# Dividing the second layer at column 256 instead of 384 in a softcap attention and soft-MoE kernel

## The chip, the cores and the metric

The kernel runs on one core of one Trainium2 chip. The metric is the device time of one execution in microseconds; several runs are taken and their median counts. Beside the runs there is one execution under the hardware profiler, whose span reaches from the first to the last instruction of the program.

## The reference

Eight batches of twelve heads run an attention with capped scores; its output, 3584 tokens of 768 columns, goes through a soft mixture of eight experts with four slots each.

```python
scores = scale * np.matmul(q, k.transpose(0, 1, 3, 2))   # 8 x 12 heads, 448 x 448, head_dim 64
scores = cap * np.tanh(scores / cap)
attn = softmax(scores)
x = (attn @ v) as [3584, 768]

logits = x @ phi                                  # 32 slots
slot_input = softmax(logits over tokens).T @ x    # 32 x 768
for e in range(8):
    h = np.maximum(slot_input[e] @ w1[e], 0.0)    # 4 x 1024
    slot_out[e] = h @ w2[e]                       # 4 x 768
out = softmax(logits over slots) @ slot_out       # 3584 x 768, float32
```

## The kernel before

The kernel writes the order of every engine out by hand. Its first part, some 236 us, is the attention in 56 chunks: scores on PE, tanh and exp on ACT (some of the exps as a polynomial on DVE), the products with v on PE, and the slot logits and slot sums batch by batch. Beside it POOL issues the loads of the weights, 64 jobs (`wjobs`, L123 to L131), one or two in a chunk at slot "b" (L849). The first 32 are w1, which stays on chip. The other 32 are w2, cut by columns into two halves of 384 (`HD`) and by rows into 16 pieces of four blocks: 11 pieces of the first half (`KEPT`) go to the on-chip tile `w2b`, and the other 21 are converted to bf16 in HBM (`w2d`), since there is no room for them until the attention's buffers are free. In `wjobs` all of `w2d` stands before `w2b`. From the end of the attention on, SP loads the 21 pieces from `w2d` into tiles `w2t` (L1047 to L1050), each as soon as the attention buffers under it are free.

The part behind the attention goes by these steps:

- `layer1` and `relu` (L1064 to L1079): the hidden layer of experts 0 to 3 and of 4 to 7, into `hb`. Four matmuls with 32 columns of weights each run side by side on PE.
- `h_transp` (L1081): eight small matmuls turn `hb` into a PSUM tile, and DVE copies it into `hpad` (L1091). Its first call serves the first 32 of the 64 blocks of layer 2, its second the last 32. The second call is made behind 16 blocks of layer 2; `widen` (L1110), which spreads the slot weights `E` of a batch for a later transpose, and `e_recips` (L745), which makes the reciprocals `winv` of two batches, stand behind it in DVE's order.
- `layer2` (L1095): 64 matmuls for the first half of the columns into the PSUM tile `so_ps0`, copied to `so[0]` by ACT (L1158), then 64 for the second half into `so_ps1`, copied to `so[1]` by DVE (L1167).
- `half_tile` (L1132): for one tile of 128 tokens the product of its transposed slot weights with one half of `so` (L1138), scaled by `winv` into a buffer `obh` by ACT or DVE in turn, and stored by SP. `NH = 10` tiles leave in two halves: the first half of eight of them is made between the matmuls of the second half of layer 2, a pair behind every second group of four blocks, so that their stores run while PE works.
- The other 18 tiles are made whole (L1185 to L1199): two matmuls of 384 columns, one scaling of 768 by ACT or DVE, and stores of two to four tiles, whose rows are contiguous in HBM over the tiles.

`bank` (L943) gives PSUM banks by the list `turns`; the buffers `hb`, `so`, `obh` and `ob` take turns in the eight 12 KB slots of w1. All stores and the loads of `w2t` go through SP's one queue.

Of the kernel before, what the change touches and what calls it, by code (L numbers as in the profile page):

```python
# [9 lines left out]
F32 = mybir.dt.float32  # L10
BF16 = mybir.dt.bfloat16
# [7 lines left out]
P = 128  # L19
HP = 64  # L20
NT = 7
DH = 64
S = 448
CH = 6
CS = 3
NG = 4
# [11 lines left out]
def kernel(  # L38
# [12 lines left out]
    B, H, _, _ = q.shape  # L51
    D = H * DH
    E = moe_w1.shape[0]
    F = moe_w1.shape[2]
    NS = moe_phi.shape[1]
    NJ = D // P
    HD = D // 2
    NFT = F // P
    cap = float(cap)
    qk_scale = 1.0 / (DH ** 0.5)  # L60
# [27 lines left out]
    winv = consts.tile([P, B // 2, NT], F32, name="winv")  # L88
# [28 lines left out]

    def load_half(dst, n0, half):
        src = w2_src(n0, 4)
        pool.dma_start(out=dst, in_=bass.AP(tensor=src.tensor, offset=src.offset + half * HD,  # L120
                                            ap=[[D, P], [F * D, 4], [1, HD]]))

    wjobs = [(load_w1, e, jh, fh) for e in range(E) for jh in range(2) for fh in range(2)]  # L123
    w2_parts = [(n0, half) for half in range(2) for n0 in range(0, len(blocks), 4)]
    w2_kept, w2_spilled = w2_parts[:KEPT], w2_parts[KEPT:]

    dram = ctx.enter_context(tc.tile_pool(name="dram", bufs=1, space=bass.MemoryType.DRAM))
    w2d = {part: dram.tile([P, 4, HD], BF16, name=f"w2d{part[0]}_{part[1]}")
           for part in w2_spilled}
# [464 lines left out]
    c0, c1, c3 = POW2  # L594
# [115 lines left out]
    es, wides = {}, {}  # L710
# [25 lines left out]
    def et_tile(bb, c):  # L736
        return (ETl if bb == B // 2 - 1 else ET4[:, bb])[:, c, :, :].rearrange("p a q -> p (a q)")
# [7 lines left out]
    def e_recips(b):  # L745

        sums = zdiag[:, b % 2, 0:NG]
        dve.tensor_reduce(sums, es[b], axis=mybir.AxisListType.X, op=ALU.add)
        to = slice(b % 2 * HP, b % 2 * HP + HP)
        for odd in range(2):  # L750
            dve.reciprocal(winv[to, b // 2, odd:NT:2],
                           sums[odd * HP:odd * HP + HP, 0:(NT + 1 - odd) // 2])
# [63 lines left out]
    for b in range(B):  # L816
        j, p = b * PER, 6 * b
# [226 lines left out]
    tl = ctx.enter_context(tc.tile_pool(name="tl", bufs=1, reuse_waits="tile"))  # L1044

    w2t = {}
    for n0, half in sorted(w2_spilled, key=lambda x: (x[1], x[0])):  # L1047
        t = tl.tile([P, 4, HD], BF16, name=f"w2t{n0}_{half}")
        sp.dma_start(out=t, in_=w2d[n0, half])
        w2t[n0, half] = t  # L1050

    hpad = tl.tile([P, E, NFT, NS], BF16, name="hpad")
    pool.memset(hpad, 0.0)
# [21 lines left out]
    def relu(eng, dst, hp):  # L1075
        if eng is act:
            act.activation(dst, hp, ACT.Relu, scale=rz)
        else:
            dve.tensor_scalar(dst, hp, rz, 0.0, ALU.mult, ALU.max)  # L1079

    def h_transp(i):  # L1081

        own = bass.AP(tensor=ident.tensor, offset=ident.offset + 16 * i,
                      ap=[ident.ap[0], [36, 4], [1, 4]])
        src = psT.tile([P, NFT, 4, 4], F32, name="hps", tag="T")
        for ft in range(NFT):
            pe.matmul(src[:, ft, :, :], hbs[i][:, ft * P:(ft + 1) * P], own,
                      start=(ft == 0), stop=(ft == NFT - 1), skip_group_check=True)
        dst = bass.AP(tensor=hpad.tensor, offset=hpad.offset + i * (4 * NFT * NS + 16),
                      ap=[hpad.ap[0], [NS, NFT], [NFT * NS + 4, 4], [1, 4]])  # L1090
        dve.tensor_copy(dst, src)  # L1091

    so_ps = []
# [10 lines left out]
    for eng, hp in zip((act, dve), first):  # L1104
        relu(eng, *hp)
    relu(act, *layer1(1, 0, 512))
    room = [wts.tile([P, HD + NG * P], BF16, name=f"so{half}", tag="w1", bufs=E) for half in range(2)]
    so = [t[:, 0:HD] for t in room]

    def widen(b):  # L1110

        wides[b] = room[b % 2][:, HD:]
        dve.tensor_copy(wides[b].rearrange("p (g a s) -> p g a s", g=NG, s=NS),
                        es[b].unsqueeze(2).to_broadcast([P, NG, P // NS, NS]))

    widen(B - 1)
    h_transp(0)
    relu(dve, *layer1(1, 512, 768))
    relu(act, *layer1(1, 768, F))
    so_ps += [bank([P, HD], name=f"so_ps{half}") for half in range(2)]  # L1120
    obs, waiting = {}, {}

    def store(n, h0, h1, src, tokens=1):
        bb, c = divmod(n, NT)
        width = (h1 - h0) * HD
        sp.dma_start(out=bass.AP(tensor=out.tensor,
                                 offset=(2 * bb * S + c) * D + h0 * HD,
                                 ap=[[NT * D, P], [1, tokens * D]] if width == D else
                                 [[NT * D, P], [D, tokens], [1, width]]),
                     in_=src)  # L1130

    def half_tile(n, half, home, eng):  # L1132

        bb, c = divmod(n, NT)
        if c == 0:
            obs[bb, half] = wts.tile([P, NT, HD], F32, name="obh", tag="w1", bufs=E)
        ob = obs[bb, half][:, c, :]
        pe.matmul(home, et_tile(bb, c), so[half], start=True, stop=True)  # L1138
        if eng == "dve":
            dve.tensor_scalar_mul(ob, home, winv[:, bb, c:c + 1])  # L1140
        else:
            act.mul(ob, home, winv[:, bb, c:c + 1])
# [4 lines left out]
        store(k, half, half + 1, obs[bb, half][:, c - (n - k):c + 1, :], n - k + 1)  # L1147
# [10 lines left out]
    act.copy(so[0], so_ps[0])  # L1158
# [8 lines left out]
    dve.tensor_copy(so[1], so_ps[1])  # L1167
    for n, eng in ((NH - 2, "act"), (NH - 1, "dve")):
        half_tile(n, 0, bank([P, HD], name="op0"), eng)
    mid.close()  # L1170


    fin = ctx.enter_context(tc.tile_pool(name="fin", bufs=3, space=PSUM, reuse_waits="tile"))
    for n in range(B // 2 * NT):
        bb, c = divmod(n, NT)
        if n == NH + 3:
            e_transp(B - 1)
        if n == NH + 5:
            e_transp(B - 2)
# [12 lines left out]
        if n % 2:  # L1192
            dve.tensor_scalar_mul(dst, op[:, :, 0:HD], winv[:, bb, c:c + 1])
        else:
            act.mul(dst, op[:, :, 0:HD], winv[:, bb, c:c + 1])
        full = n + 1 == n1 + size
        if full:
            store(n1, 0, 2, ob[:, 0:n - n1 + 1, :, :].rearrange("p t a d -> p (t a d)"),
                  n - n1 + 1)  # L1199


# [33 lines left out]
```

## Time and profile before

| | |
|---|---|
| median of 3 runs (lowest to highest) | 281.91 us (281.11 to 282.01) |
| span of the profiled execution | 279.2 us |
| busy in the span: ACT, PE, DVE, POOL | 89%, 88%, 86%, 51% |
| granted PE clock, mean | 0.985 |
| SP's queue (loads of v and w2t, all stores) | 32.02 MB, 32.6% of 16 DMA engines' span |
| POOL's queue (q, k, weights) | 35.31 MB, 80.0% |

The page gives no other time of the profiled execution than its span. Engine rows say where an engine is busy; the windows view cuts the span into stretches and gives each engine's busy time, the number of its instructions, and in the last two columns the busy share of the 16 DMA engines and their rate. Since a DMA's time is counted where its packet starts, a share can pass 1. A timeline row is a run of like instructions on one engine: start, length from the first start to the last end, line, operation, tiles with shapes, count, and in brackets the idle time ahead of it.

### The profile page before, as it was taken

What the parts mean: (1) busy time and instruction counts of PE and PEld (TensorE: products, weight loads), DVE (VectorE), ACT (ScalarE), POOL (GpSimd) and SP (SyncE); (2) the same over time, 40 slices, a digit from 0 to 9 for tenths busy, and PEclk for the clock granted to TensorE, in tenths of its full rate; (3) what the DMA queues carried; (4) which work ended last, traced back from release to release, by engine and by line L of the source; (5) the groups of instructions that cost most, each with busy time, mean ns of one, the idle gap of its engine ahead of it and who ended that gap; (6) DMA issues with size and microseconds to landing.
All of it is one profiled execution on the core that took longest, in us unless ns stands there. A gap on an engine that the chain in (4) does not pass through costs nothing.

```text
span 279.2 us, 10421 instructions
## 1 busy us (share of the span) xinstructions
PE 247.0 (88%) x4560; PEld 166.6 (60%) x4560; DVE 239.1 (86%) x473; ACT 248.6 (89%) x195; POOL 142.0 (51%) x198
## 2 busy tenths in 40 slices
PE   8898989998999999989999999899999999998720
PEld 7555556756675766566756675657566678553300
DVE  3479999999999999999999999999999997347940
ACT  4999999999999999999999999999999998237720
POOL 8796548662957296728673758375743230200000
PEclk9999999999999999999999999999999999999995
DMA  6999999999999999999999999999999588979997
GB/s 197 277 193 202 219 219 234 229 221 219 224 225 220 219 229 226 225 217 229 223 226 212 213 219 231 218 210 215 231 217 215 117 279 293 367 290 383 434 424 312
DMA packets 57340, 68.08 MB, mean 244 GB/s; under 512 B 4048, under 2 KB 53840, under 8 KB 56784
## 3 DMA queue, kind: packets, MB, share of 16 engines
q0 software_dynamic: 42448, 35.31, 80.0%
q1 hardware_dynamic: 14704, 32.02, 32.6%
q8 instruction: 35, 0.57, 0.7%
q10 hardware_dynamic: 144, 0.10, 0.1%
q14 instruction: 9, 0.07, 0.1%
HBM read 91.72 MB, written 19.27 MB: 398 GB/s over the span
## 4 chain that ended last, share of the span: by engine, by line
ACT 38%; DVE 27%; PE 27%; issue 3%; POOL 1%; ACTq 0%; DVEq 0%
ACT ex L366 15%; ACT ex L374 15%; PE pv L627 8%; ACT ex L362 6%; DVE xq L637 4%; PE sc L349 3%; DVE xp L605 3%; DVE xp L607 3%; DVE ex L608 2%; DVE ex L602 2%; PE so_ps L1098 2%; PE hp L1070 2%; DVE xf L604 2%; DVE ex L609 2%; DVE xp L606 2%
## 5 line engine op out<-in xcount | busy, mean ns | idle before, releaser
L366 ACT ACTIVATE ex<-sc 128x1344 f16<-128x1344 f32 (+1 forms) x87 | 112.9, 1402 | 0.9 <-PE sc L349 0.9
L374 ACT ACTIVATE ex<-ex 128x1344 bf16<-128x1344 f16 (+5 forms) x58 | 110.7, 1916 | 0.1
L627 PE MATMUL pv<-vbd,ex 128*128 128x130 bf16 (+1 forms) x1610 | 94.0, 212 | 7.6 <-POOL vbd L289 3.4
L627 PEld LDWEIGHTS <-ex 128*128 128x128 bf16 (+1 forms) x1680 | 75.6, 101 | 34.9 <-issue 6.2
L289 POOL CAST vbd<-vraw 64x896 bf16<-64x896 f32 x46 | 47.3, 1028 | 57.3 <-PE pv L627 35.7
L349 PE MATMUL sc<-qT,kT 64*64 64x448 bf16 x672 | 66.0, 359 | 6.7 <-ACT ex L366 4.8
L362 ACT ACTIVATE ex<-sc 128x2688 f16<-128x2688 f32 x13 | 33.6, 2586 | 0.0
L349 PEld LDWEIGHTS <-kT 64*64 64x64 bf16 x672 | 22.1, 105 | 16.3 <-ACT ex L366 6.9
L637 DVE TENSOR_TENSOR xq<-pv,rec 128x448 bf16<-128x448 f32 x46 | 28.7, 625 | 1.6
L607 DVE TENSOR_TENSOR xp<-xp,xf 128x1344 f16<-128x1344 f16 (+2 forms) x34 | 27.1, 798 | 0.6
L608 DVE TENSOR_TENSOR ex<-ex,xp 128x1344 uint16<-128x1344 uint16 (+2 forms) x34 | 26.9, 791 | 0.2
L605 DVE TENSOR_TENSOR xp<-xf 128x1344 f16<-128x1344 uint16 (+2 forms) x34 | 26.8, 789 | 0.2
L116 POOL DMA_DIRECT2D w1b<-in_moe_w_dram x32 | 26.3, 825 | 0.0
L602 DVE TENSOR_SCALAR ex<-ex 128x1344 uint16<-128x1344 f16 (+2 forms) x34 | 17.0, 500 | 1.4 <-ACT ex L366 0.8
L606 DVE TENSOR_SCALAR xp<-xp 128x1344 f16<-128x1344 f16 (+2 forms) x34 | 17.2, 505 | 0.6
L281 DVE COPY kT<-kps 128x896 bf16<-128x896 bf16 x23 | 14.2, 617 | 4.0 <-PE kps L276 2.8
L297 POOL MEMSET vbd<- 64x1 bf16 x22 | 2.8, 129 | 28.6 <-PE pv L627 28.3
L604 DVE TENSOR_SCALAR xf<-ex 128x1344 uint16<-128x1344 uint16 (+2 forms) x34 | 16.7, 491 | 0.4
L185 POOL DMA_DIRECT2D qb<-in_q_dram x22 | 16.3, 740 | 1.2 <-PE qps L279 0.5
L609 DVE TENSOR_SCALAR ex<-ex 128x1344 uint16<-128x1344 uint16 (+2 forms) x34 | 16.4, 483 | 0.4
L120 POOL DMA_DIRECT2D w2d<-in_moe_w_dram x21 | 16.4, 816 | 0.0
L185 POOL DMA_DIRECT2D kb<-in_k_dram x22 | 16.3, 739 | 0.0
(124 smaller groups left out, 320.2 us busy)
## 6 DMA issues: line engine op xcount, KB each, us to landing
w1b<-in_moe_w_dram POOLq DMA_DIRECT2D x32, 384.0 KB, 10.2
vraw<-in_v_dram SPq DMA_DIRECT2D x44, 224.0 KB, 6.2
w2d<-in_moe_w_dram POOLq DMA_DIRECT2D x21, 384.0 KB, 9.9
w2t<-w2d SPq DMA_DIRECT2D x21, 384.0 KB, 6.2
qb<-in_q_dram POOLq DMA_DIRECT2D x22, 224.0 KB, 8.2
kb<-in_k_dram POOLq DMA_DIRECT2D x22, 224.0 KB, 8.1
w2b<-in_moe_w_dram POOLq DMA_DIRECT2D x11, 384.0 KB, 9.5
out_dram<-ob SPq DMA_DIRECT2D x2, 1536.0 KB, 7.7
```

The source lines that it names most:

```text
L116: pool.dma_start(out=w1b[e][:, js, fs], in_=w1r[:, e, js, fs])
L185: pool.dma_start(out=t, in_=quad_ap(nm, Q))
L289: pool.tensor_copy(vbds[Q % 2][r, :, :, c0:c0 + DH], raw[r])
L349: ins = pe.matmul(sc[cs, u, 0:S], qkT["k", Q][r, c, cs], qkT["q", Q][r, :, cs], start=True, stop=True).ins
L362: apart["t", i - 1] = apart["t", i] = act.activation(exs[j].bitcast(F16), own["board"][:, :, 0:S], ACT.Tanh, scale=qk_scale / cap).ins
L366: ins = act.activation(exs[j][:, half * CS + u0:half * CS + u1, :].bitcast(F16), (own[0] if i == u0 == 0 else sc)[:, u0:u1, 0:S], ACT.Tanh ...
L374: act.activation(exs[j][:, u0:u1, :], exs[j][:, u0:u1, :].bitcast(F16), ACT.Exp, scale=cap)
L605: lambda: dve.tensor_tensor(p, s, s.bitcast(F16), op=ALU.mult),
L607: lambda: dve.tensor_tensor(p, p, s, op=ALU.mult),
L608: lambda: dve.tensor_tensor(y, y, p, op=ALU.add),
L627: pe.matmul(out_, exs[j][r, u, q0:q0 + (HP if tail else P)], v_, start=(c == 0 and g == gs[0] < NF), stop=(c == NT - 1), skip_group_check= ...
L637: dve.tensor_tensor(xq[Q][:, h, s0:s1, :], pv[:, 0:s1 - s0, 0:DH], rec.to_broadcast([P, s1 - s0, DH]), op=ALU.mult)
```

## The change

Layer 2 is divided at column 256: `WD` is (256, 512). The first part's 16 weight pieces all stay on chip in `w2b` (16 x 256 columns instead of 11 x 384), the second part's 16 all go through HBM (16 x 512 instead of 21 x 384), and in `wjobs` the two kinds alternate. Both parts of `so` lie side by side in one buffer, so that the whole tiles still take two matmuls of 384. Sixteen tiles (`NH`) instead of ten leave in two parts; the first parts of all sixteen are made inside layer 2's second part, a pair behind each of the groups 2 to 9; stores of both parts are made for pairs of tiles, with a buffer of seven tiles for the first part and of four for the second. The second `widen` and the two `e_recips` move ahead of layer 2, and the copy of `so_ps1` is cut between DVE and ACT.

```diff
+    CUTS = (0, D // 3, D)
+    WD = tuple(CUTS[n + 1] - CUTS[n] for n in range(2))
-    KEPT = 11
-    w2b = wts.tile([P, KEPT, 4, HD], BF16, name="w2b")
+    w2b = wts.tile([P, E * NFT // 4, 4, WD[0]], BF16, name="w2b")
...
-    wjobs += [(load_half, w2d[part], *part) for part in w2_spilled]
-    wjobs += [(load_half, w2b[:, n, :, :], *part) for n, part in enumerate(w2_kept)]
+    for n in range(len(w2_kept)):
+        wjobs.append((load_half, w2d[w2_spilled[n]], *w2_spilled[n]))
+        wjobs.append((load_half, w2b[:, n, :, :], *w2_kept[n]))
...
-    turns = [0, 1, 2, 6, 3, 4, 5, 0, 6, 0, 1, 2, 3, 6, 5, 4, 0, 1, 2, 6, 3, 0, 1, 2, 6, 5]
+    turns = [0, 1, 2, 6, 3, 4, 5, 0, 6, 0, 1, 2, 3, 6, 5, 4] + [0, 1, 2, 6, 3, 5] * 4
...
-        t = tl.tile([P, 4, HD], BF16, name=f"w2t{n0}_{half}")
+        t = tl.tile([P, 4, WD[1]], BF16, name=f"w2t{n0}_{half}")
...
-    room = [wts.tile([P, HD + NG * P], BF16, name=f"so{half}", tag="w1", bufs=E) for half in range(2)]
-    so = [t[:, 0:HD] for t in room]
+    room = [wts.tile([P, D + NG * P], BF16, name=f"so{half}", tag="w1", bufs=E) for half in range(2)]
+    so = [room[0][:, CUTS[n]:CUTS[n + 1]] for n in range(2)]
...
+    GR = (NT, 4)
-    def half_tile(n, half, home, eng):
+    def part_tile(n, half, home, eng):
...
-        if c == 0:
-            obs[bb, half] = wts.tile([P, NT, HD], F32, name="obh", tag="w1", bufs=E)
-        ob = obs[bb, half][:, c, :]
+        g, u = divmod(c, GR[half])
+        if u == 0:
+            obs[bb, half, g] = wts.tile([P, GR[half], WD[half]], F32, name="obh", tag="w1", bufs=E)
+        ob = obs[bb, half, g]
...
-        if half and 0 < n < NH - 1 and c < NT - 1 and k == n:
+        if 0 < n < NH - 1 and u < GR[half] - 1 and c < NT - 1 and k == n:
...
-    NH = 10
+    NH = 16
+    widen(B - 2)
+    for b in (B - 2, B - 1):
+        e_recips(b)
     for n0 in range(0, n2, 4):
         if n0 == n2 // 2 - 16:
             h_transp(1)
-            widen(B - 2)
-            for b in (B - 2, B - 1):
-                e_recips(b)
         layer2(n0, 0)
     act.copy(so[0], so_ps[0])
     done = 0
     for n0 in range(0, n2, 4):
         layer2(n0, 1)
-        if n0 % 8 == 4 and n0 > 4 and done < NH - 2:
+        if n0 and done < NH:
             for eng in ("act", "dve"):
-                half_tile(done, 0, bank([P, HD], name="op0"), eng)
+                part_tile(done, 0, bank([P, WD[0]], name="op0"), eng)
                 done += 1
-    dve.tensor_copy(so[1], so_ps[1])
-    for n, eng in ((NH - 2, "act"), (NH - 1, "dve")):
-        half_tile(n, 0, bank([P, HD], name="op0"), eng)
+    dve.tensor_copy(so[1][:, 0:WD[1] // 2], so_ps[1][:, 0:WD[1] // 2])
+    act.copy(so[1][:, WD[1] // 2:], so_ps[1][:, WD[1] // 2:])
...
-        if n == NH + 3:
+        if n == 13:
-        if n == NH + 5:
+        if n == 15:
...
-            half_tile(n, 1, op[:, 0, 0:HD], "dve" if n % 2 else "act")
+            part_tile(n, 1, op[:, 0, 0:WD[1]], "dve" if n % 2 else "act")
...
-            pe.matmul(op[:, half, 0:HD], et_tile(bb, c), so[half],
+            pe.matmul(op[:, half, 0:HD], et_tile(bb, c), room[0][:, half * HD:half * HD + HD],
```

The change moves instructions at three places that matter below. The first is DVE's order around the second copy into `hpad`; `hps` is the turned hidden layer, `E` the slot weights of a batch, and the COPY into a tile `so` is `widen`. Before:

```order
L1091 CAST hpad<-hps 128x8x4x4
L1079 TENSOR_SCALAR hb<-hp,rz 128x256
L1091 CAST hpad<-hps 128x8x4x4
L1113 COPY so_5878<-E 128x512
L748 TENSOR_REDUCE zdiag<-E 128x4
L751 RECIPROCAL winv<-zdiag 64x4
L751 RECIPROCAL winv<-zdiag 64x3
```

and with the change:

```order
L1092 CAST hpad<-hps 128x8x4x4
L1080 TENSOR_SCALAR hb<-hp,rz 128x256
L1114 COPY so_5863<-E 128x512
L749 TENSOR_REDUCE zdiag<-E 128x4
L752 RECIPROCAL winv<-zdiag 64x4
L752 RECIPROCAL winv<-zdiag 64x3
L749 TENSOR_REDUCE zdiag<-E 128x4
L752 RECIPROCAL winv<-zdiag 64x4
L752 RECIPROCAL winv<-zdiag 64x3
L1092 CAST hpad<-hps 128x8x4x4
```

Seven instructions that stood behind the second CAST into `hpad` now stand ahead of it; PE's matmuls of blocks 32 to 63 read what that CAST writes.

The second place is DVE's order between the two copies of layer 2's results, where `op` is the PSUM tile of a tile's product and the CAST is the copy of `so_ps1`. Before:

```order
L1140 TENSOR_SCALAR obh<-op_6048,winv 128x384
L1140 TENSOR_SCALAR obh<-op_6064,winv 128x384
L1140 TENSOR_SCALAR obh<-op_6080,winv 128x384
L1140 TENSOR_SCALAR obh<-op_6096,winv 128x384
L1167 CAST so_5879<-so_ps_5944 128x384
L1140 TENSOR_SCALAR obh<-op_6130,winv 128x384
```

and with the change:

```order
L1144 TENSOR_SCALAR obh<-op_6025,winv 128x256
L1144 TENSOR_SCALAR obh<-op_6036,winv 128x256
L1144 TENSOR_SCALAR obh<-op_6047,winv 128x256
L1144 TENSOR_SCALAR obh<-op_6058,winv 128x256
L1144 TENSOR_SCALAR obh<-op_6070,winv 128x256
L1144 TENSOR_SCALAR obh<-op_6081,winv 128x256
L1144 TENSOR_SCALAR obh<-op_6092,winv 128x256
L1144 TENSOR_SCALAR obh<-op_6104,winv 128x256
L1171 CAST so_5863<-so_ps_5929 128x256
```

Eight pairs of tiles (DVE has one of each pair, ACT the other) instead of four now stand ahead of the copy; the fifth pair before stood behind it. The third place is ACT's order around its new half of that copy, with the semaphores that each instruction waits for:

```order
L1146 ACTIVATE obh<-op_6077,winv 128x256 [waits PE_49]
L1146 ACTIVATE obh<-op_6088,winv 128x256 [waits PE_49]
L1146 ACTIVATE obh<-op_6100,winv 128x256 [waits DMASW3_49,DMASW1_49,DMASW5_49,DMASW0_49,PE_49]
L1172 CAST so_5863<-so_ps_5929 128x256 [waits DVE_49]
L1146 ACTIVATE obh<-op,winv 128x512 [waits DMASW5_49,DMASW6_49,DMASW0_49,DMASW7_49,PE_49,Pool_49]
```

ACT had no instruction here before; its half of the copy waits for DVE, whose last instruction ahead of it is the other half of the same copy.

More of the change, by code (lines that the diff above doesn't have):

```diff
@@ L119, in load_half @@
         src = w2_src(n0, 4)
-        pool.dma_start(out=dst, in_=bass.AP(tensor=src.tensor, offset=src.offset + half * HD,
-                                            ap=[[D, P], [F * D, 4], [1, HD]]))
+        pool.dma_start(out=dst, in_=bass.AP(tensor=src.tensor, offset=src.offset + CUTS[half],
+                                            ap=[[D, P], [F * D, 4], [1, WD[half]]]))
     wjobs = [(load_w1, e, jh, fh) for e in range(E) for jh in range(2) for fh in range(2)]
-    w2_parts = [(n0, half) for half in range(2) for n0 in range(0, len(blocks), 4)]
-    w2_kept, w2_spilled = w2_parts[:KEPT], w2_parts[KEPT:]
+    w2_kept, w2_spilled = ([(n0, half) for n0 in range(0, len(blocks), 4)] for half in range(2))
     dram = ctx.enter_context(tc.tile_pool(name="dram", bufs=1, space=bass.MemoryType.DRAM))
-    w2d = {part: dram.tile([P, 4, HD], BF16, name=f"w2d{part[0]}_{part[1]}")
+    w2d = {part: dram.tile([P, 4, WD[1]], BF16, name=f"w2d{part[0]}_{part[1]}")
            for part in w2_spilled}
-    wjobs += [(load_half, w2d[part], *part) for part in w2_spilled]
-    wjobs += [(load_half, w2b[:, n, :, :], *part) for n, part in enumerate(w2_kept)]
+    for n in range(len(w2_kept)):
+        wjobs.append((load_half, w2d[w2_spilled[n]], *w2_spilled[n]))
+        wjobs.append((load_half, w2b[:, n, :, :], *w2_kept[n]))
     att = ExitStack()
@@ L1106 @@
     relu(act, *layer1(1, 0, 512))
-    room = [wts.tile([P, HD + NG * P], BF16, name=f"so{half}", tag="w1", bufs=E) for half in range(2)]
-    so = [t[:, 0:HD] for t in room]
+    room = [wts.tile([P, D + NG * P], BF16, name=f"so{half}", tag="w1", bufs=E) for half in range(2)]
+    so = [room[0][:, CUTS[n]:CUTS[n + 1]] for n in range(2)]
     def widen(b):
-        wides[b] = room[b % 2][:, HD:]
+        wides[b] = room[b % 2][:, D:]
         dve.tensor_copy(wides[b].rearrange("p (g a s) -> p g a s", g=NG, s=NS),
@@ L1119, with store @@
     relu(act, *layer1(1, 768, F))
-    so_ps += [bank([P, HD], name=f"so_ps{half}") for half in range(2)]
+    so_ps += [bank([P, WD[half]], name=f"so_ps{half}") for half in range(2)]
     obs, waiting = {}, {}
-    def store(n, h0, h1, src, tokens=1):
+    def store(n, c0, c1, src, tokens=1):
         bb, c = divmod(n, NT)
-        width = (h1 - h0) * HD
+        width = c1 - c0
         sp.dma_start(out=bass.AP(tensor=out.tensor,
-                                 offset=(2 * bb * S + c) * D + h0 * HD,
+                                 offset=(2 * bb * S + c) * D + c0,
                                  ap=[[NT * D, P], [1, tokens * D]] if width == D else
@@ L1130, in store @@
                      in_=src)
-    def half_tile(n, half, home, eng):
+    GR = (NT, 4)
+    def part_tile(n, half, home, eng):
         bb, c = divmod(n, NT)
-        if c == 0:
-            obs[bb, half] = wts.tile([P, NT, HD], F32, name="obh", tag="w1", bufs=E)
-        ob = obs[bb, half][:, c, :]
+        g, u = divmod(c, GR[half])
+        if u == 0:
+            obs[bb, half, g] = wts.tile([P, GR[half], WD[half]], F32, name="obh", tag="w1", bufs=E)
+        ob = obs[bb, half, g]
         pe.matmul(home, et_tile(bb, c), so[half], start=True, stop=True)
         if eng == "dve":
-            dve.tensor_scalar_mul(ob, home, winv[:, bb, c:c + 1])
+            dve.tensor_scalar_mul(ob[:, u, :], home, winv[:, bb, c:c + 1])
         else:
-            act.mul(ob, home, winv[:, bb, c:c + 1])
+            act.mul(ob[:, u, :], home, winv[:, bb, c:c + 1])
         k = waiting.pop(half, n)
-        if half and 0 < n < NH - 1 and c < NT - 1 and k == n:
+        if 0 < n < NH - 1 and u < GR[half] - 1 and c < NT - 1 and k == n:
             waiting[half] = n
             return
-        store(k, half, half + 1, obs[bb, half][:, c - (n - k):c + 1, :], n - k + 1)
-    NH = 10
+        store(k, CUTS[half], CUTS[half + 1], ob[:, u - (n - k):u + 1, :], n - k + 1)
+    NH = 16
     n2 = len(blocks)
+    widen(B - 2)
+    for b in (B - 2, B - 1):
+        e_recips(b)
     for n0 in range(0, n2, 4):
@@ L1197 @@
         if full:
-            store(n1, 0, 2, ob[:, 0:n - n1 + 1, :, :].rearrange("p t a d -> p (t a d)"),
+            store(n1, 0, D, ob[:, 0:n - n1 + 1, :, :].rearrange("p t a d -> p (t a d)"),
                   n - n1 + 1)
```

## The prediction

> **What bounds the kernel now.** I read the engine rows first (ACT and PE are both near nine tenths until 236 us), then the chain of waits, then stretches of the tail one by one, because everything that the change rewrites on the engines lies behind 245 us. The stretches show that the tail has another limit than the attention:
>
> ```profile
> core 0: us, PE busy (x) PEld busy (x) DVE busy (x) ACT busy (x) POOL busy (x), PEclk, DMA share, GB/s
> 248.50:249.90 1.40, 1.40 (x27) 0.39 (x20) 0.29 (x1) 0.98 (x2) 0.00 (x0) 1.00 0.36 137
> 249.90:250.80 0.90, 0.90 (x15) 0.26 (x12) 0.72 (x2) 0.61 (x2) 0.00 (x0) 1.00 0.01 3
> 250.80:254.50 3.70, 3.46 (x44) 1.26 (x42) 2.64 (x6) 2.03 (x5) 0.00 (x0) 1.00 1.04 387
> 254.50:255.00 0.50, 0.16 (x2) 0.10 (x1) 0.50 (x1) 0.50 (x2) 0.00 (x0) 1.00 0.83 307
> 255.00:260.50 5.50, 4.86 (x27) 2.25 (x26) 4.90 (x10) 4.62 (x7) 0.00 (x0) 1.00 1.05 392
> 261.00:264.50 3.50, 2.45 (x14) 1.17 (x13) 2.81 (x4) 2.59 (x3) 0.00 (x0) 1.00 1.03 429
> 261.00:277.80 16.80, 4.59 (x23) 1.93 (x21) 6.45 (x7) 5.30 (x6) 0.00 (x0) 0.80 0.99 419
> 277.80:279.20 1.40, 0.00 (x0) 0.00 (x0) 0.00 (x0) 0.00 (x0) 0.00 (x0) 0.50 0.00 0
> ...
> 249.98 8.86 SPq L1126 DMA_DIRECT2D out_dram<-obh  x16
> 259.08 9.57 SPq L1126 DMA_DIRECT2D out_dram<-ob  x6
> ```
>
> The last two columns are the 16 DMA engines' busy share and rate; the last two rows are SP's store issues. The first store is issued at 249.98 and its data moves from 250.8, 0.82 us later. From there the DMA engines are full until 277.8, with one small dip at 254.5, and the span ends 1.4 us behind. Issuing ends at 268.65, so DVE, ACT and PE have some 9 us of slack at the end. The tail is therefore a stream of 11.0 MB (3584 x 768 x 4 bytes), and its end is: when it starts, plus its bytes at the rate of their pieces, plus every hole in it. That is the account in which I put the change. The page's span is 279.2 us, the runs' median 281.91; I add the difference of the spans to the median.
>
> **Rate by piece.** A stored row of a 384-column half is 1536 bytes: 392 GB/s at share 1.05, so 16 x 1536 / (392/1.05) = 65.8 ns on one DMA engine. The two-token stores of 261.0 to 264.5 have rows of 6144 bytes: 16 x 6144 / (429/1.03) = 236 ns. Two points give 9.1 ns per piece plus 0.0369 ns per byte. Estimates from that at share 1.05 and 1.04: pieces of 1024 bytes (256 columns) 46.9 ns, 367 GB/s; of 2048 bytes (512 columns) 84.7 ns, 402 GB/s. [...]
>
> **Part by part.** Weights through HBM: 21 loads of 384 KB become 16 of 512 KB, 1.6% more bytes; the buffers on chip come free at the same events.
>
> ```profile
> L1049 SPq DMA_DIRECT2D w2t<-w2d x21: 319/371/1539, 222.2 to 242.5; - x21
> DMA to landing us min/median/max: 3.0/6.2/8.5
> ...
> L120 POOL DMA_DIRECT2D w2d<-in_moe_w_dram x21: 696/774/992, 112.1 to 174.3; - x21
> L120 POOL DMA_DIRECT2D w2b<-in_moe_w_dram x11: 740/760/834, 180.5 to 212.8; - x11
> ...
> PE sc L349 <- ACT ex L366: 4.6, 9, 0.7
> PE pv L627 <- POOL vbd L289: 3.2, 7, 0.7
> ...
> PE sc L349 <- DVE qT L281: 0.4, 2, 0.3
> ```
>
> The last is issued at 242.5 and lands by 251 at the latest; its last reader now runs at about 255 (below), so PE's second part hides the loads and I cost them at nothing; without that cover each late microsecond would be one of the end. On POOL the 32 jobs stay 32 at the same places; 774 and 760 ns an issue are one price, and a job of 512 KB instead of 384 is followed by one of 256. In the attention PE's wait list (8 rows, first and last shown) names no DMA, so I cost the mixed order at nothing too, bounds -0.3 and +0.5 us, nearest to nothing.
>
> First part of layer 2, 256 columns instead of 384:
>
> ```profile
> 239.63 4.07 PE L1070 MATMUL hp<-w1b,slT 128*32 128x512 bf16 x72
> 243.92 1.49 PE L1070 MATMUL hp<-w1b,slT 128*32 128x256 bf16 x48
> ...
> 246.00 0.36 PE L1087 MATMUL hps<-ident,hb 128*128 128x16 bf16 x8
> 246.28 1.32 PE L1098 MATMUL so_ps<-w2b,hpad 128*32 128x384 bf16 x28
> 247.43 1.64 PE L1098 MATMUL so_ps<-w2t,hpad 128*32 128x384 bf16 x36
> 249.00 0.50 PE L1138 MATMUL op<-so,ET 128*128 128x384 bf16 x2
> 249.43 0.51 PE L1098 MATMUL so_ps<-w2t,hpad 128*32 128x384 bf16 x8
> 249.87 0.50 PE L1138 MATMUL op<-so,ET 128*128 128x384 bf16 x2
> 250.30 0.51 PE L1098 MATMUL so_ps<-w2t,hpad 128*32 128x384 bf16 x8
> ...
> 244.81 0.48 DVE L1079 TENSOR_SCALAR hb<-hp,rz 128x256 bf16<-128x256 f32 x1 [0.43 <-PE hp L1070]
> 246.39 0.29 DVE L1091 CAST hpad<-hps 128x128 bf16<-128x128 f32 x1 [1.10 <-PE hps L1087]
> 246.60 0.28 DVE L1113 COPY so<-E 128x512 bf16<-128x512 bf16 x1
> ...
> 247.80 0.36 DVE L751 RECIPROCAL winv<-zdiag 64x4 f32<-64x4 f32 x2
> 253.25 0.56 DVE L1167 CAST so<-so_ps 128x384 bf16<-128x384 f32 x1 [0.48 <-PE so_ps L1098]
> ...
> 248.47 0.48 ACT L1158 CAST so<-so_ps 128x384 bf16<-128x384 f32 x1 [2.53 <-PE so_ps L1098]
> 249.38 0.58 ACT L1142 ACTIVATE obh<-op,winv 128x384 f32<-128x384 f32 x1 [0.42 <-PE op L1138]
> ...
> L1077 ACT ACTIVATE hb<-hp,rz 128x512 bf16<-128x512 f32 x2 | 1.4, 688 | 4.3 <-PE hp L1070 4.3
> L1077 ACT ACTIVATE hb<-hp,rz 128x256 bf16<-128x256 f32 x1 | 0.5, 475 | 1.0 <-PE hp L1070 1.0
> ```
>
> Four matmuls run side by side as a group. With one drain of 0.16 us at the end of each run, the rows of 72, 48 and 36 matmuls give 0.217 us a group at 512 columns (18 groups), 0.111 at 256 (12) and 0.164 at 384 (9), in proportion to the columns. The second transpose at 246.00 hangs on ACT's relu and stays; behind it 12 groups are left, 12 x 0.053 = 0.64 us less. But the moved widen and reciprocals now stand ahead of DVE's CAST into hpad, which the last eight groups read. They take 246.60 to 248.16, 1.56 us, and can start when the relu ends at 245.29 (DVE is idle 1.10 us there now): to 246.85, CAST to 247.14, PE on at 247.19 instead of 246.28 + 4 x 0.111 = 246.72, a new stall of 0.47 us (bounds 0.2, if they start earlier, and 0.6). Eight groups and the drain end at 248.24; ACT's copy loses 0.11 (a third of 384 columns at the slope of ACT's two relu rows, 0.213 us per 256): 248.29 to 248.66; tile 0 starts at 248.71 instead of 249.00, its matmul ends at 248.98, ACT (475 ns) at 249.50, the store goes out at 249.52 and moves data at 250.34: **0.46 us earlier**.
>
> Second part. Before, a pair of 384-column tiles stands behind every second group, four pairs in all, and a cycle is 0.87 us (249.43 to 250.30): 2 x 0.164 for the groups, 2 x 0.17 for the tiles, 0.2 for the two changes between them. Now eight pairs stand behind single groups of 512 columns: 0.217 + 2 x 0.12 + 0.2 = 0.65 us. The eighth pair starts at 248.71 + 7 x 0.65 = 253.26, takes 0.33 (0.43 less two thirds of 0.16), seven groups follow (1.52), and the drain: so_ps is whole at **255.3 instead of 253.25**. Bounds for the changes: nothing (0.45 a cycle, 1.6 us less) and what an old cycle costs (0.87, 1.5 more); the price of the old changes is nearest, as the same two matmul shapes meet.
>
> The copy in two. DVE's 256 columns take 0.56 less 0.11, by ACT's slope, ACT's 0.48 less 0.11; as the order shows, ACT's half waits for DVE's, so with two hops the pair is 0.9 us, not 0.45 (the two bounds). [...] Then: tile 0 of the second part at 256.2, matmul 0.38, ACT 0.69 (688 ns), issued 257.3, **data at 258.15**.
>
> The hole. The first part is 16 x 128 KB = 2.10 MB: 5.7 us at 367 GB/s, and 0.25 lost behind the lone first store (the next needs another cycle). From 250.34 it runs dry at **256.3**. Before, ten larger pieces (1.97 MB) reached to 255.8 and the next came in time. So the engines idle 1.85 us. Behind it lie 16 x 256 KB at 402 GB/s, 10.4 us, and 12 whole tiles, 4.72 MB at 419 GB/s, 11.3 us: 279.85, and 1.4 to the span's end: 281.25. ACT writes a tile of 512 columns in 0.69 us beside DVE, while a pair's stores last 1.3 us, so nothing starves again; the slack of 9 us shrinks by two. SP's 23 stores instead of 22 cost nothing: 16 of them took 8.86 us, 0.55 each, under the 0.7 us or more of data in a pair. Buffers that are written again wait for stores issued at least six before them, which the hole lets land.
>
> **Sum against 279.2:** start -0.46, hole +1.85 instead of about 0.1, lone-store gap +0.25, pieces (5.7 + 10.4 + 11.3 = 27.4 against 26.9) +0.5: **+2.0 us**. The hops between engines are rounded up, so I take +1.9: 281.91 + 1.9 = **283.8 us**.
>
> **Rivals.** (1) The stream stays whole: PE changes between shapes for nothing and the weights of so come 1.85 us earlier. Then 250.34 + 0.25 + 27.4 + 1.4 = 279.4, **282.1 us**: no change. For it: the old dip was only 0.5 us long. Against it: the 0.87 us cycles. (2) Faster: the stream is whole and small pieces cost no more, so 27.0 us count from 250.34: 278.7, **281.4 us**; this mechanism needs the second part's first data by 256.3 and is decided there. [...] (3) The larger HBM loads come late, or the mixed order delays k and q: the last load must come over 4 us after 251 to matter, and the end moves by as much as it passes 255; with the +0.5 of the mixed order and 1.2 of lateness **285.5 us**. (4) The cycle stays at 0.87: so_ps at 256.8, **285.3 us**.
>
> **Chances.** Forecast 0.70, rival (1) 0.12, (2) 0.08, (3) 0.05, (4) 0.05. What a measurement here can tell from no change is about 0.3%, 0.85 us. Faster 0.09, same 0.15 (rival 1 and the forecast's lower edge), slower 0.76. Own range of the forecast 282.9 to 284.8; with rival (1) and part of (4) it reaches from 282.1 to 285.1.
>
> **What would show it.** In the changed profile: first store issued near 249.5; the first part's CAST into hpad near 246.9 with PE idle before it; so_ps whole near 255.3; the two copies one behind the other; and a stretch of DMA share near nothing between 256.3 and 258.1. If the share stays at one through 258, rival (1) or (2) holds and I am wrong; if the hole is there but the end is not later, my rates by piece are.

## The result, and the profile after

| | before | changed |
|---|---|---|
| median of 7 runs each (lowest to highest) | 281.90 us (281.10 to 282.01) | 283.12 us (282.79 to 283.63) |
| ratio of the medians, with its 95% interval | | 1.0052 (1.0036 to 1.0069) |
| span of the profiled execution | 279.2 us | 281.2 us |
| start of layer 1's first matmul | 239.63 us | 239.50 us |
| first store issued, its data from | 249.98, 250.82 us | 249.36, 250.20 us |
| stream of stores empty: last packet ahead starts, next one starts | not | 256.28, 258.09 us |
| last packet of a store ends | 277.81 us | 279.60 us |

The changed kernel is slower by 1.2 us, 0.5%, and the forecast of 283.8 lay 0.7 too high. The two profiled spans differ by 2.0. (Starts and ends of packets are from the traces' packet records; the stretches below bracket them.)

First the stretches of the changed kernel's tail, with the same columns as the stretches of before; the last two are the share of the 16 DMA engines and their rate.

```profile
248.50:249.90 1.40, 1.36 (x15) 0.51 (x14) 0.76 (x2) 0.86 (x2) 0.00 (x0) 1.00 0.14 59
249.90:250.80 0.90, 0.90 (x12) 0.27 (x8) 0.69 (x2) 0.56 (x2) 0.00 (x0) 1.00 0.46 164
250.80:254.50 3.70, 3.70 (x45) 1.41 (x48) 2.42 (x5) 2.37 (x5) 0.00 (x0) 1.00 1.05 369
...
256.30:258.00 1.70, 1.31 (x6) 0.46 (x5) 1.07 (x2) 1.30 (x3) 0.00 (x0) 1.00 0.00 0
258.10:261.00 2.90, 2.27 (x8) 0.67 (x7) 2.69 (x5) 2.59 (x4) 0.00 (x0) 1.00 1.04 400
261.00:264.50 3.50, 3.17 (x19) 1.48 (x18) 3.31 (x6) 2.48 (x5) 0.00 (x0) 1.00 1.05 408
261.00:277.80 16.80, 6.98 (x36) 3.01 (x34) 8.45 (x11) 6.69 (x9) 0.00 (x0) 0.79 1.04 424
277.80:279.60 1.80, 0.00 (x0) 0.00 (x0) 0.00 (x0) 0.00 (x0) 0.00 (x0) 0.50 0.82 348
279.60:281.20 1.60, 0.00 (x0) 0.00 (x0) 0.00 (x0) 0.00 (x0) 0.00 (x0) 0.50 0.00 0
```

The reader is to see three things: data moves earlier than before (share 0.46 in 249.90 to 250.80, where before had 0.01), the DMA engines stand still for the whole of 256.30 to 258.00 (the hole), and behind that they are full to 279.6, where before ended at 277.8.

The timeline of the same kernel shows why the stream runs dry: PE, DVE and ACT around the two places that were rewritten.

```profile
246.01 0.62 PE L1099 MATMUL so_ps<-w2b,hpad 128*32 128x256 bf16 x16
247.02 1.06 PE L1099 MATMUL so_ps<-w2b,hpad 128*32 128x256 bf16 x32 [0.39 <-DVE hpad L1092]
247.90 0.60 PE L1099 MATMUL so_ps<-w2t,hpad 128*32 128x512 bf16 x8
248.55 0.38 PE L1142 MATMUL op<-so,ET 128*128 128x256 bf16 x2
...
253.12 0.39 PE L1142 MATMUL op<-so,ET 128*128 128x256 bf16 x2
253.44 1.70 PE L1099 MATMUL so_ps<-w2t,hpad 128*32 128x512 bf16 x28
256.07 0.81 PE L1142 MATMUL op<-so,ET 128*128 128x512 bf16 x3 [0.93 <-ACT so L1172]
...
246.67 0.29 DVE L1092 CAST hpad<-hps 128x128 bf16<-128x128 f32 x1
255.19 0.42 DVE L1171 CAST so<-so_ps 128x256 bf16<-128x256 f32 x1 [1.16 <-PE so_ps L1099]
...
255.64 0.37 ACT L1172 CAST so<-so_ps 128x256 bf16<-128x256 f32 x1 [1.73 <-DVE so L1171]
256.53 1.27 ACT L1146 ACTIVATE obh<-op,winv 128x512 f32<-128x512 f32 x2 [0.51 <-PE op L1142]
```

PE waits 0.39 us for the CAST into hpad; from the first pair of tiles (248.55) to the eighth (253.12) it takes seven cycles of 0.65; so_ps1 is whole at 255.19 instead of 253.25, two copies follow one behind the other to 256.01, and the first 512-column tile is scaled from 256.53 to 257.2. Its store's data comes at 258.09, 1.81 us after the last packet of the sixteen first parts started.

### The profile page after: what moved, and what is told of

Same layout as the page of the kernel before. It is cut to its first block, busy times and chain, and to the rows that moved or that the text cites. A ratio compares the mean times of both kernels' runs of the same rounds, so it can differ in the third digit from the quotient of the medians.

```text
span 281.2 us, 10422 instructions
## 1 busy us (share of the span) xinstructions
PE 248.3 (88%) x4560; PEld 166.6 (59%) x4560; DVE 239.5 (85%) x476; ACT 249.7 (89%) x199; POOL 141.9 (50%) x198
## 4 chain that ended last, share of the span: by engine, by line
ACT 44%; PE 26%; DVE 21%; issue 4%; POOL 1%; DVEq 0%; ACTq 0%
ACT ex L375 17%; ACT ex L367 17%; PE pv L628 8%; ACT ex L363 7%; PE sc L350 3%; DVE xq L638 3%; DVE xp L606 2%; DVE xp L608 2%; PE op L1142 2%; PE so_ps L1099 2%; DVE ex L603 2%; PE hp L1071 2%; DVE xf L605 2%; DVE ex L609 2%; DVE ex L610 1%
## 5 line engine op out<-in xcount | busy, mean ns | idle before, releaser
L690 DVE COPY xT<-xps 128x896 bf16<-128x896 bf16 (+1 forms) x24 | 14.3, 594 | 1.0 <-PE xps L681 1.0
```

## The experiments

All times of the tail are counted from layer 1's first matmul, since the attention ahead of it ends at 239.3 to 240.4 us from one execution to the next, which hides steps of a few tenths in the medians (the kernel with the old order of the weights, below, ends it far later). "Tail" is from there to the end of the last store packet; "second part" is the first packet of a store of a second part, which has rows of 2048 bytes. A kernel's median is of all its runs, 4 to 12; its ratio is against the runs of the kernel before on the same chip, whose medians were 281.4 to 281.9.

| kernel | first store | stream empty | second part | tail | median, ratio to before (interval) |
|---|---|---|---|---|---|
| before, first trace | 10.35 | not | | 38.18 | 281.90 |
| changed | 9.86 | 1.81 | 18.59 | 40.10 | 283.12, 1.0052 (1.0036 to 1.0069) |
| reciprocals back | 9.52 | 1.55 | 18.24 | 39.76 | 283.26, 1.0049 (1.0025 to 1.0074) |
| one copy | 9.97 | 1.25 | 18.59 | 40.10 | 283.37, 1.0069 (1.0055 to 1.0083) |
| four tiles at a time | 9.85 | 1.01 | 17.71 | 39.22 | 282.56, 1.0031 (1.0011 to 1.0051) |
| ten tiles in two parts | 9.86 | 2.33 | 17.23 | 40.49 | 283.62, 1.0074 (1.0047 to 1.0100) |
| column 384, sixteen tiles | 10.36 | not | | 38.57 | 282.65, 1.0030 (1.0008 to 1.0051) |
| three at once | 9.57 | 0.25 | 17.30 | 38.81 | 282.26, 1.0028 (1.0009 to 1.0047) |

The two columns "second part" and "tail" belong together: from the second part's first packet to the end it takes 21.5 us in every kernel here with sixteen tiles at column 256. The length of the empty stretch alone says less. With one copy it is 0.56 shorter than in the changed kernel at the same tail, because the sixteen first parts begin 0.1 us later there and take 6.57 us from first packet to last, instead of 6.13; why they take longer stays open.

**The start.** `widen` and the reciprocals go back behind the CAST into hpad.

```diff
-    widen(B - 2)
-    for b in (B - 2, B - 1):
-        e_recips(b)
     for n0 in range(0, n2, 4):
         if n0 == n2 // 2 - 16:
             h_transp(1)
+            widen(B - 2)
+            for b in (B - 2, B - 1):
+                e_recips(b)
```

> The change with the second widen and the two e_recips put back behind the second hidden transpose in DVE's order. Theory (the store stream has a hole of about 1.9 us because the second part of so comes late, and the end is that moment plus the bytes left): PE's 0.4 us wait for the CAST into hpad goes, everything behind it comes 0.4 us earlier, the hole keeps its length, and the time is 0.4 us under the change's: 282.7 us. Rival (the loss lies in the smaller stored pieces alone): no difference, 283.1.

The first store comes 0.34 us earlier after layer 1's start and the tail is 0.34 shorter: the wait for the CAST is worth what it lasts, less 0.05 us. The median, 283.26, does not show it beside 283.12: the end of the attention scatters by more (240.14 in this trace, 239.50 in that of the change).

**The hole.** Four tiles behind every second group of four blocks, in place of two behind every group: the same matmuls, half the changes between the two kinds.

```diff
-        if n0 and done < NH:
-            for eng in ("act", "dve"):
+        if n0 % 8 == 4 and done < NH:
+            for eng in ("act", "dve") * 2:
```

> The change with four tiles behind every second group of layer 2's second part instead of two behind every group. The matmuls are the same, the changes between the two shapes on PE are 4 instead of 8. Theory: 4 x 0.2 = 0.8 us less until the second part is whole, the hole shrinks by that, 282.3 us. Rival (pieces): the same pieces, 283.1.

The stretches of this kernel across the hole:

```profile
255.00:256.20 1.20, 0.81 (x3) 0.29 (x3) 0.27 (x1) 0.69 (x2) 0.00 (x0) 1.00 1.09 383
256.30:257.30 1.00, 0.80 (x3) 0.29 (x3) 0.76 (x2) 0.83 (x3) 0.00 (x0) 1.00 0.00 1
257.40:260.50 3.10, 2.47 (x11) 0.82 (x9) 2.89 (x5) 2.55 (x4) 0.00 (x0) 1.00 1.06 407
```

The stream runs dry at the same time and stays empty for 1.0 us instead of 1.8. The second part's first packet comes 0.88 earlier, and the tail is 0.88 shorter. Eight changes fewer between the 32-column groups and the tiles would account for it at 0.11 us each, an estimate from this difference alone: the view shows no idle time of PE at the changes.

**Pieces or hole.** Ten tiles in two parts instead of sixteen at column 256 takes small pieces away and leaves less to send ahead of the second part; sixteen at column 384 does the reverse to the kernel before (there the list of banks is lengthened to match; only the edit for ten tiles is shown).

```diff
-    NH = 16
+    NH = 10
```

> The change with 10 tiles in two parts instead of 16. Theory: three pairs fewer ahead of the second part bring it 3 x 0.43 = 1.3 us earlier, but only 3.6 us of first-part data bridge the time until then, the hole grows to about 2.7 us, and behind it lie 6.5 us of second parts and 16.9 of whole tiles instead of 10.4 and 11.3: 0.8 us over the change, 283.9 us. Rival (smaller pieces cost the time): six tiles fewer in pieces, 0.6 us under the change, 282.5.

> The kernel before with 16 tiles in two halves of 384 instead of 10. Theory: seven pairs instead of four stand ahead of the second half, which comes 1.6 us later, but the first halves now last 8 us, so the stream has no hole; only the smaller pieces of six more tiles cost, 0.65 us by the rates: 282.5 us. Rival (the number of tiles in two parts is the cost at any division): as the change, 283.1.

With ten tiles the hole is 2.33 us and the tail 0.39 longer: had the small pieces been what costs, six tiles fewer of them would have made it shorter. The expected 0.8 is a slip in its own sum. Its terms, a second part 1.3 us earlier and 23.4 us behind it instead of 21.7, give 0.4, and 1.36 earlier with 23.25 behind it was measured.

With sixteen tiles at column 384 the stream never runs dry. The runs put this kernel 0.2 to 1.4 us above before, and the expected 0.65 lies in that. The traces do not show it: its tail of 38.57 lies among those of three traces of before (38.18 to 38.88, further down), and from first store to last packet it takes 28.22 us, where those take 27.83 to 28.04. What the smaller pieces and three more pairs cost here stays open between nothing and that.

**The copy.**

```diff
-    dve.tensor_copy(so[1][:, 0:WD[1] // 2], so_ps[1][:, 0:WD[1] // 2])
-    act.copy(so[1][:, WD[1] // 2:], so_ps[1][:, WD[1] // 2:])
+    dve.tensor_copy(so[1], so_ps[1])
```

> The changed kernel with so_ps1 copied by DVE alone in one instruction. Theory: the halves of the copy run one behind the other (0.84 us from DVE's start to ACT's end in the trace of the change), one copy of 512 columns takes 0.56 + 0.11 to 0.15 = 0.67 to 0.71 us; from layer 1's first matmul to the last packet 40.10 - 0.15 = 39.95 us, the hole 1.65. Rival: the halves could overlap if DVE were not late, so one copy costs 0.27 us more: 40.4, hole 2.1.

PE's rows of this kernel, at the start of layer 2's second part and at the copy:

```profile
247.91 0.81 PE L1099 MATMUL so_ps<-w2t,hpad 128*32 128x512 bf16 x8
...
256.04 0.82 PE L1142 MATMUL op<-so,ET 128*128 128x512 bf16 x3 [0.80 <-DVE so L1171]
```

The wait for the copy falls from 0.93 to 0.80, so the cut in two had cost 0.13 and gained nothing. But the eight matmuls at 247.91 took 0.81 instead of 0.60, which puts all that follows 0.1 later, and the second part's first packet and the tail came out the same. The expected 0.15 is seen at its place and not in the sum. Since ACT's half waits for DVE's in the changed kernel (DVE's ends at 255.61, ACT's starts at 255.64), what two halves at once would take was not shown.

**Three at once.** The reciprocals, the one copy and the four tiles together.

> The changed kernel with three parts altered at once: widen and the reciprocals back behind the CAST into hpad, so_ps1 copied by DVE alone, and four first-part tiles behind every second group instead of two behind every group. Theory: the single gains add, 0.34 and 0.88 as measured alone and 0.15 as expected: from layer 1's first matmul to the last packet 40.10 - 1.37 = 38.7 us, the hole about 0.5 to 0.85, the time about 282.0; still not faster than before (38.18), since the hole and the smaller pieces remain. Rival: the gains hide one another (each only fills the same hole), then 39.2 and 282.5.

Stretches of this kernel:

```profile
249.70:254.50 4.80, 4.10 (x57) 1.62 (x56) 3.18 (x7) 2.31 (x6) 0.00 (x0) 1.00 0.84 296
254.50:256.30 1.80, 1.31 (x5) 0.50 (x6) 0.86 (x3) 1.22 (x2) 0.00 (x0) 1.00 1.09 382
256.30:256.70 0.40, 0.40 (x2) 0.10 (x1) 0.40 (x1) 0.23 (x2) 0.00 (x0) 1.00 0.21 72
256.70:260.50 3.80, 3.17 (x14) 1.12 (x13) 3.54 (x7) 3.19 (x5) 0.00 (x0) 1.00 1.05 406
```

and DVE's row of its first tiles in the timeline:

```profile
248.58 1.89 DVE L1144 TENSOR_SCALAR obh<-op,winv 128x256 f32<-128x256 f32 x4 [0.88 <-PE op L1142]
```

The gains add: tail 38.81, where 38.7 was expected, and of the 1.92 us between the changed kernel and the first trace of before 1.29 are back. The hole is down to 0.25. The first stretch still shows a weak start, share 0.84 in 249.70 to 254.50, where DVE scales its first four tiles one behind the other in 1.89 us. It is not what is left of the loss: the end still stands 21.5 us behind the second part's first packet, and a denser start would only empty the stream sooner. To end with the first trace of before, that packet would have to come 0.63 us earlier still. The kernel is still 0.28% slower than before, so the runs show no gain from the division at column 256, even with its three weak places mended.

**The order of the weights.** The prediction put the mixed order of the weight loads at no cost. The next kernel keeps everything of the change but that order:

```diff
-    for n in range(len(w2_kept)):
-        wjobs.append((load_half, w2d[w2_spilled[n]], *w2_spilled[n]))
-        wjobs.append((load_half, w2b[:, n, :, :], *w2_kept[n]))
+    wjobs += [(load_half, w2d[part], *part) for part in w2_spilled]
+    wjobs += [(load_half, w2b[:, n, :, :], *part) for n, part in enumerate(w2_kept)]
```

> The changed kernel with the weight jobs in the old order: all pieces that go through HBM first, then all that stay on chip. Theory: the mixed order costs nothing; layer 1 starts at 239.5 to 240.2 as in all other kernels and the time is that of the change within 0.3 us, 283.1. Rival: the mixed order delays the attention or layer 2 and hides in the scatter of layer 1's start; then it starts at 239.2 or earlier and the time is 282.6 or less.

Both theories were wrong: 292.67 us, ratio 1.0403 (1.0373 to 1.0434). Layer 1 starts at 248.80, 9.3 us late, and its tail is 40.11, the change's own. The view of the transfers issued in 110 to 185 us (count, size, median us to landing), for this kernel:

```profile
w2d<-in_moe_w_dram POOLq DMA_DIRECT2D x16, 512.0 KB, 16.0
kb<-in_k_dram POOLq DMA_DIRECT2D x7, 224.0 KB, 12.8
```

and for the changed kernel:

```profile
w2d<-in_moe_w_dram POOLq DMA_DIRECT2D x11, 512.0 KB, 11.1
w2b<-in_moe_w_dram POOLq DMA_DIRECT2D x11, 256.0 KB, 10.2
kb<-in_k_dram POOLq DMA_DIRECT2D x8, 224.0 KB, 8.7
```

The unmixed kernel where it loses the time, by stretches (the third figure from the end is PE's granted clock):

```profile
160.00:165.50 5.50, 5.26 (x123) 4.09 (x119) 5.38 (x10) 5.50 (x6) 2.24 (x3) 1.00 1.21 234
165.50:172.20 6.70, 0.49 (x14) 0.06 (x3) 1.36 (x3) 4.62 (x3) 2.78 (x4) 0.81 1.23 214
172.20:179.80 7.60, 7.56 (x107) 5.49 (x109) 4.83 (x9) 2.50 (x2) 3.15 (x4) 0.50 1.26 216
179.80:185.00 5.20, 4.43 (x83) 2.73 (x84) 4.47 (x9) 4.00 (x4) 3.57 (x5) 0.98 1.29 199
```

and PE's timeline at the end of the second of them:

```profile
172.24 0.53 PE L279 MATMUL kps<-ident,kb 128*64 128x128 bf16 x6 [6.25 <-DMA kb<-in_k_dram]
```

Sixteen pieces of 512 KB one behind the other, where before had 384 KB, fill a set of DMA engines that is already full (share 1.25 in 110 to 185 us, in before and in the changed kernel): the loads of k wait behind them, from 8.7 to 12.8 us in the median, and in the end PE stands 6.25 us for one of them. Then its granted clock is 0.50 for 7.6 us, of which PE is busy for 7.56. On this trace's chain of waits four matmuls of the scores (L349) take 0.75 us at 179.09, and 0.38 at 154.07 with the clock at 1.00. At half speed throughout, the 7.56 would be up to 3.8 us more, an estimate, and the two together cover the 9.3.

Two kernels ask whether it is the bytes that run up, or the neighbourhood of two pieces that go through HBM: blocks of four, and of eight, of each kind in turn.

```diff
+    for n in range(0, len(w2_kept), 4):
+        wjobs += [(load_half, w2d[part], *part) for part in w2_spilled[n:n + 4]]
+        wjobs += [(load_half, w2b[:, m, :, :], *w2_kept[m]) for m in range(n, n + 4)]
```

> The changed kernel with the weight jobs in blocks: four pieces that go through HBM, then four that stay on chip, and so on. With all 16 pieces through HBM in a row layer 1 began 9.3 us later; the theory formed from that trace: bytes decide. The 16 DMA engines are full all through the attention, so each 512 KB piece where 384 KB stood leaves some 0.85 us of backlog (the landing of the fourth of them 3.3 us later than in before, of the eighth 7 us), each 256 KB piece takes as much away, and the loads of k, which come 1.9 us or more ahead of their use in before, are late only once the backlog passes that lead. After four pieces the load of k at 127 us, with 3.7 us of lead, is just in time, and then the block of small pieces pays back: layer 1 at 239.4 to 240.2, at most 0.5 us late, time 283.1 to 283.6. Rival: pieces through HBM that stand next to one another disturb each other, whatever their bytes on average: 12 of 15 neighbours remain, so 9.3 x 12 / 15 = 7.4 us late, time 290.5.

> The same in blocks of eight. By bytes: the backlog reaches some 7 us at the end of a block, in the second of which the loads of k and q at 160 to 184 us have 4 to 9 us of lead; those with the least are late by about 3: layer 1 at 242.5 (240 to 244), time 286 (283.5 to 287.5). By neighbours: 14 of 15 remain, 8.7 us late, time 291.8. Were the mixed order without any use here, both this run and that in blocks of four would be at 283.1.

Blocks of four: layer 1 at 240.36, tail 40.10, 283.95 us (1.0073, 1.0054 to 1.0091), 0.35 above what the bytes had let expect at most. Blocks of eight: 239.42, tail 40.11, 283.09 us (1.0058, 1.0030 to 1.0085). Neighbours are out, as that would have put both above 290. By bytes it is the blocks of eight that miss: 286 was expected, and no delay came. The records of issue and landing of single loads show why. In the unmixed kernel the load of k issued at 156.2 us took 16.0 us to land. In before the same load took 8.1 and lay ready 1.8 us before PE took it (its lead), so 16.0 - 8.1 - 1.8 = 6.1 us are left to wait, and PE waited 6.25. In blocks of eight that load, which has the least lead of those of k, finds the run-up paid back by the small pieces and lands in 8.1 again. The tightest ones there are those issued at 126.6 and 189.0 us: they take 3.8 and 5.1 us longer than in before, where they had 3.7 and 5.3 to spare, and land less than 0.1 us ahead of PE. So a backlog costs what it exceeds the lead by, and the missed forecast had put the backlog at loads that no longer meet it. The slower clock came on top of the long wait in the unmixed kernel. That blocks of four came out 0.9 us slower than blocks of eight is explained by neither theory.

**Before, traced again.** The profiled spans of before and changed differ by 2.0 us, the medians by 1.2. Two more traces of the kernel before ask which of the two is the size of the change.

> The kernel before, unchanged, for a second trace of it. Theory: what differs between two executions of one program is when the attention ends (the start of layer 1's first matmul, 239.63 in the first trace, 239.50 to 240.15 in the five other kernels, which share the attention); from that matmul to the last store packet it takes 38.2 +- 0.15 us again. Rival: the first trace of before caught an unusually short tail, which is why the two profiled spans differ by 2.0 us and the medians by 1.2; then it takes 38.6 or more here, and its stream of stores shows a hole.

> The kernel before, unchanged, for a third trace of it. From layer 1's first matmul to the last store packet its first trace took 38.18 us and its second 38.88, with a PE wait of 0.40 us in the second that the view puts down to nothing else that it shows. Theory: PE waits there in some executions for its own next instructions; then this trace lies at one of the two, or between them if the wait is shorter, and nothing else in the tail differs. Rival: the stream of stores itself runs at another rate from one execution to the next; then the tail differs behind 250 us as well, by more than 0.2 us from first store to last packet (27.83 us in the first trace, 27.95 in the second).

The tails are 38.88 and 38.53, after 38.18 in the first trace; medians 281.35 in 12 runs beside 281.43 of the other runs of the same kernel, and one run of 281.11 for the third. The second trace's PE rows:

```profile
247.18 1.15 PE L1098 MATMUL so_ps<-w2t,hpad 128*32 128x384 bf16 x24
248.73 0.67 PE L1098 MATMUL so_ps<-w2t,hpad 128*32 128x384 bf16 x12 [0.40 <-issue]
249.33 0.50 PE L1138 MATMUL op<-so,ET 128*128 128x384 bf16 x2
```

In the first trace these 36 matmuls are one row of 1.64 us; here PE pauses 0.40 us in the midst of them and waits for nothing that the view shows ("issue"), and the first store follows 10.93 us after layer 1's start instead of 10.35. In the third trace the row of 36 lasts 1.77, and the first store follows after 10.49. From first store to last packet the three traces have 27.83, 27.95 and 28.04 us, so the stream itself also varies, by 0.2; a hole is in none of them. The first trace, the one that the prediction was made from, has the shortest tail of the three.

## Why the prediction was right, and where it was off

**What bounds the tail**, a stream of 11.0 MB with its start, its rates and its holes, held in every kernel: the second part's first packet came at 17.30 to 18.59 us, and the end 21.5 us behind it in all eight traces with sixteen tiles at column 256 (the three kernels with another order of the weights among them). Where the stream had no hole, the tail was near that of before.

**The start.** First store 249.52 forecast, 249.36 measured. The stall that the moved reciprocals cause was put at 0.47 us and is 0.39; undone, it gave 0.34.

**The second part.** Cycle 0.65 forecast and 0.65 measured; so_ps1 whole at 255.3 forecast, DVE's copy starts at 255.19; the two copies 0.9 forecast, 0.82 measured, one behind the other as the order of ACT had shown. The sixteen first parts took 6.1 us from first packet to last, 5.95 forecast, and what lies behind the hole 21.5, 21.7 forecast. Rival (4), a cycle of 0.87, is out.

**The hole.** Forecast from 256.3 to 258.15, 1.85 us; measured 256.28 to 258.09, 1.81. With it rivals (1) and (2), which need a whole stream, are out.

**The rates.** 367 and 402 GB/s forecast for pieces of 1024 and 2048 bytes; the stretches show 369 and 408 at share 1.05, and single packets on one engine last 46.0 and 84.2 ns (46.9 and 84.7 forecast). That is 0.0449 and 0.0411 ns a byte, not the one price that rival (2) needs.

**The sum.** +2.0 us between the two spans forecast, 279.2 to 281.2 measured, and +1.92 from layer 1's start to the last packet. That it agrees to a tenth is in part luck: against the second and the third trace of before the changed kernel's tail is longer by 1.22 and 1.57.

**The size, 0.7 us too large.** The step that was off is the last one, "I add the difference of the spans to the median". It took the profiled execution of before to be a middling one, 281.91 - 279.2 = 2.7 us below its time. Seven runs of the changed kernel with a span of their own lie 1.7 to 2.1 us above that span, and so do the two new traces of before (281.44 and 279.7; 281.11 and 279.3). Of 63 runs of before that have a span on record 61 lie 1.7 to 2.1 us above it as well, and two 2.6 and 2.75. So the execution on the page most likely stands for some 281.0 us, 0.9 under the median; its own time is not on record. Against the mean tail of the three traces of before, 38.53, the change costs 40.10 - 38.53 = 1.57 us, within the 1.0 to 1.9 that the interval of the ratio allows.

**The mixed order at nothing** was right for this change and had the wrong ground. The price of an issue on POOL, 774 and 760 ns, decides nothing; the transfers do. Without the mixed order the larger pieces would have cost 9.3 us, and rival (3) had it the wrong way round: it is not the mixed order that delays k but its absence. The prediction should have set the backlog from the larger pieces against the leads of the loads behind them on POOL's queue. That the larger loads of `w2t` are hidden did hold: no wait of PE for them in the changed kernel's tail.

## What to carry to other kernels

Where a stream of stores ends a kernel, starting it earlier is worth nothing if the next part then comes late: the changed kernel's first store came 0.49 us earlier after layer 1's start, and its tail was 1.92 us longer. Behind a hole the end is the next part's first data plus the bytes that are left (21.5 us of them in each of eight traces). Put the time at which the first part runs dry beside that of the second part's first data before anything else. Larger pieces on a queue that was always full here (109% of the DMA engines' time in 110 to 185 us) needed smaller ones between them: sixteen of 512 KB in a row put layer 1 9.3 us late, and mixed with those of 256 KB, or in blocks of eight, they cost it nothing. What counted is how far the bytes ran ahead before they were paid back, against the lead of each load queued behind. What stayed within the lead cost nothing (by less than 0.1 us in blocks of eight), and what passed it was waited for (6.1 us past it, 6.25 waited). And take the profiled execution's own time into the sum, not the median, when a few tenths of a per cent are at stake.

## What was not expected of the hardware

A pause of PE of 6.25 us was followed by a granted clock of 0.50 for 7.6 us in the unmixed kernel, with PE busy in all but 0.04 of them. The mean clock of 0.81 in 165.50 to 172.20 is half a clock for the last 2.5 us, so it fell some 3.7 us behind the end of PE's last matmul at 165.98, an estimate from these two figures. It was 0.51 on the mean of 178 to 180 us and 1.00 on that of 180 to 185, so it came back some 7.7 us behind PE's first matmul at 172.24. What sets these times is not shown.

PE's pause of 0 to 0.40 us in the midst of one run of matmuls goes with the time at which a transfer of 16,384 bytes on the queue that the profile's list of DMA queues calls "instruction" starts: 5.99, 6.49 and 7.12 us after layer 1's start in the three traces of before, with a first store at 10.35, 10.49 and 10.93. The eight matmuls of 0.81 us in the kernel with one copy go with 6.56, those of 0.60 in the changed kernel with 5.57. The kernel with sixteen tiles at column 384 sits at the edge: 6.45, and no pause, where 6.49 went with one of 0.13. That PE there waits for its next instructions fits these, and no run was made that tells it from another cause.
